# Redrawing the order of batch 0's scores, exponentials and global products in a hand-written list

## The chip, the cores and the metric

The kernel runs on one core of one Trainium2 chip. The metric is device time in microseconds; the kernel before is told by the median of five runs. A separate execution was taken with the hardware profiler, and every view of a profile below is of that one execution.

## The reference, cut to what matters

An attention of a Longformer kind is followed by an MLP of a ResMLP kind. There are 8 batches of 576 tokens, 8 heads of 64, and 8 global tokens. Every token sees the tokens within 32 of it and the global ones; a global token sees all.

```python
def _attn_ref(q, k, v, global_idx):
    scores = scale * np.matmul(q, k.transpose(0, 1, 3, 2))
    mask = np.abs(pos[:, None] - pos[None, :]) <= window      # window = 32
    mask = mask | is_global[:, None] | is_global[None, :]
    scores = np.where(mask, scores, -1000000000.0)
    ...                                                       # softmax
    return np.matmul(attn, v)

def _moe_ref(x, alpha1, beta1, w_tok, alpha2, beta2, w_ch1, w_ch2, lam):
    a1 = alpha1 * x + beta1
    tok = np.einsum('ts,bsd->btd', w_tok, a1)
    u = x + lam * tok
    a2 = alpha2 * u + beta2
    ch = np.maximum(a2 @ w_ch1, 0.0) @ w_ch2
    return u + lam * ch
```

## The kernel before, in words

The work falls into batches for the attention and into nine groups of 512 rows for the MLP. From the first MLP group on, matmuls of the MLP are the base of TensorE's program and the attention and token mixing of later batches are woven in between. Batch 0 has no MLP to be woven into. Its whole attention, its token mixing, and much of the loading and filling are drawn in one order written out by hand: the string `FIRST` (line 45), a list of words. A loop (line 1025) goes through the words and issues each word's instructions at once. Each engine runs its own instructions in the order of the list; a wait arises wherever an operand or a PSUM bank isn't ready. A word with a colon names the PSUM bank (0 to 7) that it writes.

Heads are worked in four pairs, 0 to 3; "third pair" is pair 2. The words, with the pair as a digit `h`:

- `z{h}{u}:bank` only names a bank; `s{h}{u}:bank` issues the score matmuls of half `u` (`sc0_mm`, line 353) into that bank and the one of `z`: ten matmuls for `u` 0, eight for `u` 1. The first half needs windows 0 to 4, the second 5 to 8.
- `e{h}{u}{a}`: the exponential on ScalarE (line 364) of head `a` of the pair, 344 columns for `u` 0, 272 for `u` 1.
- `gk1:bank`, `gk0:bank`: scores of the global keys against all queries of the four pairs (`gk0_mm`, line 300), four matmuls each; `eg1`, `eg0`: their exponentials (line 306); `G`: two VectorE products (line 278) that make the rows `G` from these and the mask `GM`. `GMa`, `GMb` fill that mask (line 857).
- `pg{h}`: two VectorE products (line 326) that pick the global queries' probabilities from the exponentials; `pt{h}`: two more (line 333) that mask the window's probabilities. Both need all four exponentials of the pair.
- `q{h}:bank`: the global query product, five matmuls (line 381); `ra{h}` on ScalarE (line 386) and `rd{h}` on VectorE (line 390) turn its result into `RG`.
- `pvx{h}`, `pvy{h}`: the PV matmuls of query tiles 0 to 2 and 3 to 4 (`pv_mms`, line 403). Each output starts with a matmul of `G` and `RG`. `nx{h}`, `ny{h}`: their normalisation on VectorE (lines 422 and 429) or, for some pairs, `nr` and `ny` on VectorE and ScalarE (line 459). `xl{h}`, `xm{h}`: scaling by alpha and lambda, on GpSimd but for pair 3 (lines 447, 464 and 465).
- `va1`, `vb1`, `va2`, `vb2`: VectorE copies of V to an odd offset (lines 936 to 939).
- `la` (GpSimd, line 963), `lb:bank` (two float32 matmuls), `lc` (ScalarE, line 965): the row lambda times alpha, spread over the partitions. The scaling needs `lc`.
- `ab:bank`, `abe`: a transpose of eight rows (line 907) and three small VectorE copies (lines 915 to 917).
- `wt{k}:bank`, `we{k}`: transposes of the token weight (line 869) and their copies by ScalarE (line 873). `rs:bank`, `re`: the token weight's row sums, which need all five.
- `sp:n`: n spare matmuls into bank 7, whose result nobody reads (line 821).
- `qtt` and `ktt`: copies of the last 64 tokens' queries (VectorE, line 684) and keys (ScalarE, line 674), which a pair's second half and `gk1` need. `b1t`: two loads of batch 1 issued by GpSimd; `pz0`, `v1f`, `qz0`, `qz1`: fills on GpSimd; `u0`: a load of batch 1's V issued by GpSimd; `beta`: a product of one row on GpSimd (line 863).

The word lists are turned into instructions by these lines:

```python
for w in FIRST.split():
    n, _, b = w.partition(":")
    if n == "sp":
        spare(int(b))
    elif b:
        hb[n] = banks[int(b)]
        ops[n](hb[n])
    else:
        ops[n]()
```

Of the kernel before, what the change touches and what calls it, by code (L numbers as in the profile page):

```python
# [44 lines left out]
FIRST = """  # L45
kgz vez io ktz pgz gb1 gbm:0 W0 gbc ar0 pz1 ar1 gath ck0 ar2 pgc tk0:1 sp:3 cq0 mask idn tq0:2 sp:16 V0 pz3
qv0 V1 pz2 cq1 V2 tq1:3 kt0 cq2 V3 tq2:4 sp:1 ck2 qv1 qv2 ck1 ck3 tk2:5 V4 kt2 tk1:6 wki cq3 gat1 kt1 tk3:0 wi
kt3 gx tq3:2 ct qv3 gt:1 tt:3 sp:3 ge0 ge1 gte fz ktt GMa qtt z20:4 s20:5 gk1:6 e201 e200 z21:0 z11:2 s11:1
gk0:3 b1t la eg1 va1 GMb s21:5 e111 z00:4 s00:6 eg0 z10:1 sp:2 va2 e210 s10:3 vb1 e211 z01:0 sp:2 e001 s01:5
e100 lb:6 e011 pz0 e010 pg2 G z31:1 s31:5 lc v1f qz0 qz1 u0 pt2 ab:0 abe sp:2 e310 q2:6 e000 wt1:1 ra2 wt3:4  # L50
sp:2 we1 pg0 rd2 pvx2:6 e101 vb2 pt0 e311 pvy2:1 e110 q0:3 nx2 we3 wt0:5 pg1 ra0 wt2:2 nr2 ny2 we0 wt4:6 xl2
rd0 we2 q1:4 pt1 z30:1 s30:5 pvx0:3 we4 xm2 pvy0:2 nx0 ra1 rs:6 e300 beta rd1 e301 nr0 pg3 pvy1:1 re pvx1:3
ny0 pt3 xl0 q3:4 tm2:5 ra3 nr1 ny1 kc0 kc1 rd3 xm0 u1 nx1 pvy3:6 pvx3:2 ad2 xl1 tm0:4 nx3 xm1 u2 u3 u4 nr3 ad0
ny3 qc0 qc1 tx2:3 tm1:5 xl3 xm3 tx0:4 ad1 bm0 tm3:6 ut0 ut2 tx1:5 ad3 ut1 bm1 bm2 tx3:4 gc1 ut3 kc2 kc3 b1i
qc2 qc3 bm3 W1s bme
"""
PLACE = {t: (g, j) for g, ts in enumerate(GROUPS) for j, t in enumerate(ts)}

# [1091 lines left out]
```

## Time and profile before

| what | value |
|---|---|
| median of 5 runs | 390.28 us (386.78 to 391.09) |
| profiled execution, its own time | 388.55 us |
| its span | 386.6 us |
| TensorE busy | 374.9 us, 97% of the span |
| VectorE busy | 227.8 us, 59% |
| ScalarE busy | 175.2 us, 45% |
| GpSimd busy | 206.8 us, 53% |
| first matmul of the MLP | at 38.67 us |
| mean granted TensorE clock | 0.996 |

PE is TensorE, PEld its weight loads, DVE VectorE, ACT ScalarE, POOL GpSimd and SP SyncE. In a row of a timeline the first number is the start and the second the time from the first start to the last end of the instructions merged in it; their count is behind the x. What stands in brackets at the end is the idle time of the engine before them and what ended it. Instructions of one engine overlap at their ends, so that the next can start before the row is over.

### The profile page before, as it was taken

The numbers are of one execution on the slowest core, as the hardware profiler recorded it, in microseconds if no ns is written. First come the engines' busy times: TensorE is split into PE (matmuls) and PEld (weight loads), VectorE is DVE, ScalarE is ACT, GpSimd is POOL, SyncE is SP. The second block draws the span as 40 slices with busy tenths as digits, with TensorE's granted clock in tenths as the row PEclk, the third lists the DMA queues.
The fourth block names the chain that finished last, engine by engine and source line by source line (L and its number), as shares of the span: only waits on it lengthen the run. The fifth ranks groups of instructions, "written<-read, shape, count | busy, mean of one in ns | idle before, by whom it ended". The sixth has DMA issues, their size and how long they took to land.

```text
span 386.6 us, 8189 instructions
## 1 busy us (share of the span) xinstructions
PE 374.9 (97%) x3120; PEld 209.2 (54%) x3120; DVE 227.8 (59%) x589; ACT 175.2 (45%) x350; POOL 206.8 (53%) x268
## 2 busy tenths in 40 slices
PE   6799999999999999999999999999999999999996
PEld 4469565546654665456545664466456654444443
DVE  6988567984477557945595559545864554014023
ACT  6786874008800881067305740386028700731720
POOL 7988647289458944894388647963241345000000
PEclk9899999999999999999999999999999999999999
DMA  8999999959979994999497999799240013101002
GB/s 258 179 228 265 211 182 153 195 81 172 140 144 137 142 167 98 117 158 144 110 128 130 146 145 104 128 151 146 82 110 1 3 56 81 42 20 62 29 27 81
DMA packets 160836, 47.87 MB, mean 124 GB/s; under 512 B 147537, under 2 KB 154521, under 8 KB 160798
## 3 DMA queue, kind: packets, MB, share of 16 engines
q0 software_dynamic: 98288, 17.05, 63.1%
q1 hardware_dynamic: 61518, 29.18, 35.7%
q10 hardware_dynamic: 992, 1.13, 1.0%
q8 instruction: 24, 0.39, 0.4%
q14 instruction: 14, 0.11, 0.1%
HBM read 38.90 MB, written 9.44 MB: 125 GB/s over the span
## 4 chain that ended last, share of the span: by engine, by line
PE 88%; DVE 7%; ACT 3%; issue 1%; POOL 1%; ACTq 0%; DVEq 0%
PE bank L127 86%; DVE XR L583 1%; DVE OT L582 1%; POOL UB L508 1%; DVE QP L239 1%; DVE XR L429 1%; ACT UT L621 1%; ACT KT L639 1%; DVE XR L503 1%; PE bank L635 0%; PE bank L901 0%; ACT HT L567 0%; DVE QP L645 0%; ACT L742 0%; DVE PGQ L326 0%
## 5 line engine op out<-in xcount | busy, mean ns | idle before, releaser
L127 PE MATMUL bank<-UT,W 128*128 128x512 bf16 x576 | 159.3, 379 | 0.0
L127 PE MATMUL bank<-W,HT 128*128 128x512 bf16 (+2 forms) x592 | 140.1, 373 | 0.0
L567 ACT ACTIVATE HT<-bank,bias 128x512 bf16<-128x512 f32 x128 | 87.9, 687 | 52.3 <-PE bank L127 51.5
L368 ACT ACTIVATE E<-bank 128x416 f16<-128x416 f32 (+1 forms) x84 | 41.8, 513 | 114.7 <-PE bank L127 113.9
L127 PEld LDWEIGHTS <-HT 128*128 128x128 bf16 (+1 forms) x610 | 54.4, 98 | 53.8 <-issue 1.9
L447 POOL TENSOR_TENSOR XL<-XR,LA 128x384 bf16<-128x384 f32 x29 | 29.1, 1003 | 74.1 <-DVE XR L429 52.2
L127 PEld LDWEIGHTS <-W 128*128 128x128 bf16 (+1 forms) x658 | 51.6, 97 | 25.5
L582 DVE TENSOR_TENSOR OT<-bank,LAM 128x512 f32<-128x512 f32 (+2 forms) x37 | 24.9, 673 | 53.8 <-PE bank L127 53.6
L508 POOL TENSOR_TENSOR UB<-XR,A 128x512 bf16<-128x512 f32 x28 | 35.8, 1288 | 24.9 <-DVE XR L503 14.3
L127 PE MATMUL bank<-RG,G 128*128 128x65 f16 x320 | 42.9, 193 | 1.3 <-DVE RG L390 1.3
L127 PE MATMUL bank<-XL,wtT 128*128 128x512 bf16 (+2 forms) x240 | 41.6, 326 | 0.0
L127 PE MATMUL bank<-Ve,PT 128*128 128x65 f16 x300 | 41.1, 194 | 0.0
L127 PEld LDWEIGHTS <-PT 128*128 128x128 f16 x540 | 30.8, 98 | 17.5 <-issue 1.1
L127 PEld LDWEIGHTS <-G 128*128 128x128 f16 x320 | 30.7, 97 | 15.2 <-DVE RG L390 0.9
L127 PEld LDWEIGHTS <-KT 128*128 128x128 bf16 (+1 forms) x324 | 23.4, 100 | 20.2 <-issue 3.5
L223 POOL DMA_DIRECT2D Ve<-in_v_dram x40 | 34.2, 877 | 0.2
L127 PE MATMUL bank<-Vo,PT 128*128 128x65 f16 x240 | 33.4, 192 | 0.0
L216 POOL DMA_DIRECT2D Kb<-in_k_dram x30 | 27.0, 899 | 4.0 <-DMA W<-in_moe_w_ch_dram 3.9
L127 PE MATMUL bank<-QP,KT 128*128 128x144 bf16 (+1 forms) x252 | 28.7, 223 | 0.4 <-DVE QP L251 0.3
L216 POOL DMA_DIRECT2D Qb<-in_q_dram x30 | 26.8, 895 | 4.2 <-DMA W<-in_moe_w_ch_dram 3.7
L583 DVE TENSOR_TENSOR XR<-OT,XR 128x512 f32<-128x512 f32 (+2 forms) x33 | 27.3, 827 | 1.6
L127 PEld LDWEIGHTS <-wtT 128*128 128x128 bf16 (+1 forms) x240 | 18.7, 99 | 17.6 <-issue 1.7
(160 smaller groups left out, 413.8 us busy)
## 6 DMA issues: line engine op xcount, KB each, us to landing
out_dram<-XR SPq DMA_DIRECT2D x31, 256.0 KB
W<-in_moe_w_ch_dram POOLq DMA_DIRECT2D x4, 1024.0 KB, 15.1
Vo<-Ve SPq DMA_DIRECT2D x12, 260.0 KB
Ve<-in_v_dram POOLq DMA_DIRECT2D x24, 128.0 KB, 5.2
Kb<-in_k_dram POOLq DMA_DIRECT2D x24, 128.0 KB, 6.4
Qb<-in_q_dram POOLq DMA_DIRECT2D x24, 128.0 KB, 6.4
Ve<-in_v_dram POOLq DMA_DIRECT2D x16, 96.0 KB, 5.1
XR<-in_k_dram SPq DMA_DIRECT2D x2, 512.0 KB
```

Of the source, the lines that this page charges most:

```text
L127: nc.tensor.matmul(out=o, lhsT=l, rhs=r, start=st, stop=sp, skip_group_check=True)
L216: nc.gpsimd.dma_start(out=dst[0:n, c, :].rearrange("p (h d) -> p h d", d=D), in_=src[b, :, c * P : c * P + n, :].rearrange("h p d -> p h d"))
L223: nc.gpsimd.dma_start(out=Ve[b % 2][r0 : r0 + hi - lo, c, :, 0:D], in_=v[b, :, lo:hi, :].rearrange("h p d -> p h d"))
L239: nc.vector.tensor_copy(out=QP[r, hp, a, :, 0:64], in_=QT[r, hp, 0:S].rearrange("p (t j) -> p t j", j=64))
L368: nc.scalar.activation(out=eb(b, hp)[:, UOFF[u] : UOFF[u + 1]], in_=ps[:, 0:n], func=AF.Exp, bias=0.0, scale=0.125)
L429: nc.vector.tensor_tensor(out=xo, in0=pv[:, :, :, 0:64], in1=rb, op=ALU.mult)
L447: xl_eng(b, hp).tensor_tensor(out=XL[b % 2][:, 0:3, cs], in0=XR[:, base : base + 3, cs], in1=lb, op=ALU.mult)
L503: nc.vector.tensor_tensor(out=x, in0=ps, in1=x, op=ALU.add)
L508: nc.gpsimd.tensor_tensor(out=ub, in0=x, in1=A2, op=ALU.mult)
L567: nc.scalar.activation(out=HT[:, ec, :], in_=st[ec], func=AF.Relu, bias=b_, scale=1.0)
L582: nc.vector.tensor_tensor(out=ot, in0=ps, in1=LAM[:, lo:hi], op=ALU.mult)
L583: nc.vector.tensor_tensor(out=x, in0=ot, in1=x, op=ALU.add)
```

## The change

Only the list `FIRST` is changed, between `s20` and the transposes of the token weight. The third pair's second half of scores is drawn ahead of the global keys' scores, and its exponentials, `pg2`, `q2`, `ra2` and `rd2` ahead of the other pairs' later work; its PV is drawn ahead of `lb`, `ab` and the token weight's transposes. The first half of pair 1's scores moves up behind `s20`. Several words have other banks. The spare matmuls of this part are five instead of eight. From `wt0` on, the list is the same but for `nr2` and `ny2`, which now stand earlier.

```diff
-kt3 gx tq3:2 ct qv3 gt:1 tt:3 sp:3 ge0 ge1 gte fz ktt GMa qtt z20:4 s20:5 gk1:6 e201 e200 z21:0 z11:2 s11:1
-gk0:3 b1t la eg1 va1 GMb s21:5 e111 z00:4 s00:6 eg0 z10:1 sp:2 va2 e210 s10:3 vb1 e211 z01:0 sp:2 e001 s01:5
-e100 lb:6 e011 pz0 e010 pg2 G z31:1 s31:5 lc v1f qz0 qz1 u0 pt2 ab:0 abe sp:2 e310 q2:6 e000 wt1:1 ra2 wt3:4
-sp:2 we1 pg0 rd2 pvx2:6 e101 vb2 pt0 e311 pvy2:1 e110 q0:3 nx2 we3 wt0:5 pg1 ra0 wt2:2 nr2 ny2 we0 wt4:6 xl2
-rd0 we2 q1:4 pt1 z30:1 s30:5 pvx0:3 we4 xm2 pvy0:2 nx0 ra1 rs:6 e300 beta rd1 e301 nr0 pg3 pvy1:1 re pvx1:3
+kt3 gx tq3:2 ct qv3 gt:1 tt:3 sp:3 ge0 ge1 gte fz ktt GMa qtt z20:4 s20:5 e201 e200 z10:0 s10:2 e101 e100 b1t
+la z21:6 s21:1 va1 e211 e210 GMb gk1:5 eg1 gk0:4 eg0 va2 pg2 z11:0 s11:2 e111 e110 vb1 z00:6 s00:1 q2:3 ra2 G
+e001 e000 z01:5 s01:4 pt2 rd2 pz0 sp:2 pvx2:0 vb2 pvy2:2 e011 e010 z31:6 s31:1 v1f e311 e310 nx2 nr2 ny2 lb:3
+lc ab:5 abe pg0 qz0 qz1 u0 sp:3 wt1:0 wt3:4 we1 pt0 we3 q0:3 wt0:5 pg1 ra0 wt2:2 we0 wt4:6 xl2 rd0 we2 q1:4
+pt1 z30:1 s30:5 pvx0:3 we4 xm2 pvy0:2 nx0 ra1 rs:6 e300 beta rd1 e301 nr0 pg3 pvy1:1 re pvx1:3 ny0 pt3 xl0
```

More of the change, by code (lines that the diff above doesn't have):

```diff
@@ L47 @@
 qv0 V1 pz2 cq1 V2 tq1:3 kt0 cq2 V3 tq2:4 sp:1 ck2 qv1 qv2 ck1 ck3 tk2:5 V4 kt2 tk1:6 wki cq3 gat1 kt1 tk3:0 wi
-kt3 gx tq3:2 ct qv3 gt:1 tt:3 sp:3 ge0 ge1 gte fz ktt GMa qtt z20:4 s20:5 gk1:6 e201 e200 z21:0 z11:2 s11:1
-gk0:3 b1t la eg1 va1 GMb s21:5 e111 z00:4 s00:6 eg0 z10:1 sp:2 va2 e210 s10:3 vb1 e211 z01:0 sp:2 e001 s01:5
-e100 lb:6 e011 pz0 e010 pg2 G z31:1 s31:5 lc v1f qz0 qz1 u0 pt2 ab:0 abe sp:2 e310 q2:6 e000 wt1:1 ra2 wt3:4
-sp:2 we1 pg0 rd2 pvx2:6 e101 vb2 pt0 e311 pvy2:1 e110 q0:3 nx2 we3 wt0:5 pg1 ra0 wt2:2 nr2 ny2 we0 wt4:6 xl2
-rd0 we2 q1:4 pt1 z30:1 s30:5 pvx0:3 we4 xm2 pvy0:2 nx0 ra1 rs:6 e300 beta rd1 e301 nr0 pg3 pvy1:1 re pvx1:3
-ny0 pt3 xl0 q3:4 tm2:5 ra3 nr1 ny1 kc0 kc1 rd3 xm0 u1 nx1 pvy3:6 pvx3:2 ad2 xl1 tm0:4 nx3 xm1 u2 u3 u4 nr3 ad0
-ny3 qc0 qc1 tx2:3 tm1:5 xl3 xm3 tx0:4 ad1 bm0 tm3:6 ut0 ut2 tx1:5 ad3 ut1 bm1 bm2 tx3:4 gc1 ut3 kc2 kc3 b1i
-qc2 qc3 bm3 W1s bme
+kt3 gx tq3:2 ct qv3 gt:1 tt:3 sp:3 ge0 ge1 gte fz ktt GMa qtt z20:4 s20:5 e201 e200 z10:0 s10:2 e101 e100 b1t
[3 more added lines that the diff above has]
+pt1 z30:1 s30:5 pvx0:3 we4 xm2 pvy0:2 nx0 ra1 rs:6 e300 beta rd1 e301 nr0 pg3 pvy1:1 re pvx1:3 ny0 pt3 xl0
+q3:4 tm2:5 ra3 nr1 ny1 kc0 kc1 rd3 xm0 u1 nx1 pvy3:6 pvx3:2 ad2 xl1 tm0:4 nx3 xm1 u2 u3 u4 nr3 ad0 ny3 qc0 qc1
+tx2:3 tm1:5 xl3 xm3 tx0:4 ad1 bm0 tm3:6 ut0 ut2 tx1:5 ad3 ut1 bm1 bm2 tx3:4 gc1 ut3 kc2 kc3 b1i qc2 qc3 bm3
+W1s bme
 """
```

## The prediction

> **What bounds the kernel now.** I read the page first, then the chain that ended last, then a table of windows cut at the edges of the slow stretch of the clock, then the timelines of TensorE, VectorE and GpSimd from 13 to 30 us, where the change lies. The page and the chain say that TensorE is the end-setter nearly everywhere:
>
> ```profile
> span 386.6 us, 8189 instructions
> PE 374.9 (97%) x3120; PEld 209.2 (54%) x3120; DVE 227.8 (59%) x589; ACT 175.2 (45%) x350; POOL 206.8 (53%) x268
> ...
> PE 88%; DVE 7%; ACT 3%; issue 1%; POOL 1%; ACTq 0%; DVEq 0%
> ```
>
> So only TensorE's idle or half-clock time can be won, and a delay on another engine counts only where TensorE runs dry. From 100 us on, TensorE is busy 283.2 of 286 us, and nothing there is edited; a shift made before 30 us should travel to the end roughly one for one. What the edited stretch looks like is in the windows (first column start:end, then its length, then busy time of PE, PEld, DVE, ACT, POOL with instruction counts, then granted clock):
>
> ```profile
> 11.52:14.93 3.41, 1.91 (x25) 1.26 (x23) 3.09 (x9) 2.26 (x7) 3.30 (x11) 0.99 2.91 148
> 14.93:18.35 3.42, 3.42 (x44) 1.65 (x44) 3.19 (x5) 1.96 (x6) 3.40 (x5) 0.51 1.21 213
> 18.35:21.76 3.41, 3.41 (x51) 2.06 (x48) 2.30 (x11) 2.88 (x9) 3.19 (x8) 1.00 1.06 219
> 21.76:25.17 3.41, 2.99 (x65) 2.61 (x63) 3.19 (x13) 3.41 (x9) 2.17 (x3) 1.00 1.06 229
> ```
>
> A slice in which TensorE is busy 1.91 of 3.41 us (56%) is followed by one at half clock; slices at 2.9 of 3.41 (86%) are not. The reader should also see that VectorE has 2.3 to 3.2 of 3.4 us of work: it is the second bound. TensorE's gaps are few:
>
> ```profile
> 14.70 1.10 PE L127 MATMUL bank<-W,KGP 128*128 128x320 bf16 x4 [1.12 <-DVE W L684]
> ...
> 24.31 0.41 PE L869 MATMUL bank<-C,HT 96*64 96x96 bf16 x6 [0.36 <-DVE XR L429]
> ...
> 27.99 0.20 PE L127 MATMUL bank<-RG,G 128*128 128x65 f16 x1 [0.44 <-DVE RG L390]
> ```
>
> VectorE decides each of them:
>
> ```profile
> 14.68 0.71 DVE L936 COPY Vo<-Ve 64x1560 f16<-64x1560 f16 x1
> ...
> 16.50 1.59 DVE L937 COPY Vo<-Ve 64x1560 f16<-64x1560 f16 x1
> 18.26 0.31 DVE L326 TENSOR_TENSOR PGQ<-W,gqm 128x80 f16<-128x80 f16 x2 [0.17 <-ACT W L364]
> 18.49 0.82 DVE L278 TENSOR_TENSOR G<-EG,GM 128x1024 f16<-128x1024 f16 x2
> 19.23 0.82 DVE L333 TENSOR_TENSOR HT<-W,mask 128x640 f16<-128x640 f16 x2
> ...
> 28.18 1.27 DVE L326 TENSOR_TENSOR PGQ<-W,gqm 128x80 f16<-128x80 f16 x2
> ```
>
> The copy vb1 (L937) takes 1.59 us where its twin va1 (L936) takes 0.71, and the same pair of L326 products takes 0.31 or 1.27. The long ones lie under tensor products on GpSimd (`la`, 16.41 to 17.67 us; L447, 27.98 to 28.98 us).
>
> **The change, part by part.** No instruction is new; three of the eight spare matmuls of this stretch go. GpSimd's own order (b1t, la, pz0, v1f, qz0, qz1, u0, xl2) is the same before and after, and so is SP's: b1t's two DMAs and u0's are moved in the list, but past nothing on their queue. What is reordered is TensorE, ScalarE and VectorE.
>
> (1) s10 into the gap. Pair 1's first ten score matmuls (18.20 to about 18.48) go right behind s20, whose matmuls start at 13.07 and take 0.51. They need only what s20 needed, so they run at 13.4 to 13.9, inside the 1.12 us gap. s21 then takes the place of gk1 at 14.70, behind the same copy (qtt, L684). Gain on TensorE 0.3.
>
> (2) Scores of pair 2 ahead of the global keys. s21's eight matmuls at full clock are done by 15.05; the exponentials go at the steps seen on ScalarE (0.35 for 344 columns, 0.28 for 272): e201 at 13.88, e200, e101, e100, then e211 at 15.28, e210 done at 15.95 instead of about 18.2. gk1 and gk0 follow at 14.92 to 16.9 (their own 1.07 and 0.9 at half clock), so eg0 ends at 17.4 instead of 17.5.
>
> (3) VectorE. va1, GMb, va2 stay and end at 16.48. pg2 now comes before vb1, and starts at 16.50 under `la`. Its cost is 0.31 to 1.27 by the two rows; vb1 then has 0.71 of work, of which the row of 1.59 shows that about 0.3 gets done in 1.17 us under `la`. Either way vb1 ends at 18.1 to 18.4, which is where it ended before (18.09). So G starts at 18.2 to 18.45 (18.49 before) and pt2 ends at 19.8 to 20.05 (20.05 before). **This is the step at which the gain goes**: e210 is over 2 us earlier, yet G and pt2 are not, for VectorE's queue was the later one.
>
> (4) TensorE to the PV. s11 and s00 take 16.85 to 17.9, q2 0.5 at half clock to 18.4, s01 and sp:2 to 18.95. ra2 (0.37) is done at 18.9, rd2 follows pt2 and ends at 20.1 to 20.4. pvx2's first matmul waits for rd2, and all of TensorE behind it: s31, lb, ab, wt1. New idle time 1.15 to 1.45 us, where there was none. The PV starts at 20.1 to 20.4 instead of 22.15.
>
> (5) From the PV to pair 0's PV. Start-to-start steps of the rows of before: pvx2 and pvy2 0.85, s31 0.23, lb 1.05, ab 0.16, sp:3 0.48, wt1 and wt3 0.61, q0 0.27, wt0 and wt2 0.61, wt4 0.35, q1 0.47, s30 0.33: 5.41 in all. So pvx0 comes at 25.5 to 25.8, against 25.46. The 0.36 gap before wt4 is gone, since pvx2 no longer shares bank 6 with it. ScalarE adds a little: its five wide weight copies (0.53 each) now start at about 23.6 behind wt1, not at 21.58, so we4 ends at 26.35 to 26.8, and rs, which needs it, starts at 26.5 to 26.85 instead of 26.31. That is 0.2 to 0.55 late. Behind rs, TensorE before waited 0.44 us for rd1, which hides most of this; ScalarE's `re` and ny0 end up to 0.5 later.
>
> (6) VectorE behind it. nx2 and ny2 (about 1.45 together) now run at 20.9 to 22.6, but pg0 waits for abe, abe for ab, ab for lb: pg0 at 22.8 to 23.1, pt0 to 24.7 at worst, rd0 (behind ra0 and the late we1, we3) at 24.85 to 25.2, against 25.11. xl2 on GpSimd starts at about 23.2 instead of 24.43, so it lies under pt0, and `beta` lies under pt1 as xm2 did. pt1, nx0, rd1 and pg3 come out where they were, within 0.25 us.
>
> **Sum.** TensorE: 1.12 gap mostly filled, 0.36 gap removed and 0.4 of spares gone, but idle 1.3 new, and pair 0's chain 0 to 0.55 later: I take +0.3, the middle. Against the profiled execution's own 388.55 us (span 386.6 and 1.95 around it) that is 388.85. The median of the five runs is 1.73 above that execution, so on the scale of the runs 390.28 + 0.3 = 390.6. The runs spread by 4.3 us, or 1.1%; so about 1% (3.9 us) is what such a measurement can tell from no change.
>
> **The clock.** The unknown is whether the new 1.3 us stall makes a second half-clock slice. In 18.35 to 21.76 TensorE would be busy about 2.0 of 3.41 us (58%), next to the 56% that was punished and far from 86% that was not. The price is bounded by 0.17, the wait that the present half-clock slice shows on VectorE, and 1.71, half of 3.41, if TensorE sets the end throughout; lb, ab and the transposes are a chain through TensorE, so I take 1.4. On the other side s10 raises the first slice from 1.91 to about 2.3 busy; if it then stays at full clock, little is won, since vb1 on VectorE ends at 18.1 anyway.
>
> The Trainium skill ("TensorE: Matmul & The Clock Gate", section on HAM oscillation) speaks of TensorE gaps over about 3.4 us as what sends the clock down. This trace disagrees: its longest gap is 1.12 us and the clock still halved. By the page the new stall would be free of it, and the sum would stay at 390.6; by the row it may be 392.0.
>
> **Rivals.**
> A, forecast, chance 0.50: the stall moves and nothing is won: 390.6, own range 389.4 to 391.9 (0 to 0.55, with nearly 1 us for the median of five).
> B, slower, 0.27: the stall at 18.95 to 20.3 sends the clock to half from 21.8 to 25.2. For it: 58% against 56%. Against: the threshold may be just between, and the slices start at a different place in each run. It decides once rd2 comes later than about 20 us. 390.6 + 1.4 = 392.0, at most 392.4.
> C, faster, 0.16: vb1 and pg2 are not stretched by `la`, so vb1 ends at 17.55, G and pt2 come 0.6 to 0.9 earlier, and rs comes at 25.9. For it: va1's 0.71. Against: `la` starts behind b1t at 16.41 in both. The weight copies then also come early: 390.6 - 1.1 = 389.5.
> D, it doesn't do what it says, 0.07: rd2 is held until 22.1, so the PV isn't earlier, and the lb, s31 and transposes behind it are later: 22.15 + 5.41 = 27.56 for pvx0, 2.1 late: 392.4.
>
> The range takes in B's upper end and C with the spread of a median: 388.3 to 393.4. Over 1% needs a second cause on top (two extra slow slices, or a disturbed stretch after 40 us): 0.13 slower, from B and D; 0.06 faster, from C; 0.81 within.
>
> **What would show it.** A TensorE gap of over 1 us ahead of the first RG,G matmul, released by RG L390, with that matmul at 20.1 to 20.4; G at 18.2 to 18.5; the L873 copies starting at about 23.6; rs (wtT,ones) at 26.5 to 26.9; q3 within 0.5 of 29.50. Half clock at 21.8 to 25.2 is B. G before 17.9 is C. I am wrong if W1's first MLP matmul (38.67) moves by over 2 us, or if it doesn't and the time does.

## The result, and the profile after

The changed kernel takes 391.21 us (median of 38 runs, 389.68 to 393.49), the kernel before 388.89 us (median of 75 runs beside these). The ratio is 1.0054, 95% interval 1.0041 to 1.0067: slower by some 2.1 us, clear of noise and within 1%. (The difference of the medians is 2.3; the ratio is not the quotient of the medians.) The forecast of 390.6 stood on the five runs known then, whose median of 390.28 was 1.4 above that of the 75; as a difference it was +0.3, and +2.1 came.

The head of the page of the changed kernel, profiled execution 391.94 us:

```profile
span 390.0 us, 8182 instructions
PE 375.9 (96%) x3117; PEld 210.6 (54%) x3117; DVE 228.8 (59%) x589; ACT 175.4 (45%) x350; POOL 207.3 (53%) x268
```

The span is 3.4 us longer, and TensorE's busy time only 1.0, with three matmuls fewer. TensorE's timeline shows where it stood still:

```profile
15.88 0.61 PE L127 MATMUL bank<-W,KT 64*128 64x64 bf16 x18
18.47 0.44 PE L127 MATMUL bank<-Ve,PGQ 128*128 128x130 f16 x5 [1.98 <-DVE PGQ L326]
18.85 0.30 PE L127 MATMUL bank<-W,KT 64*128 64x64 bf16 x8
19.08 0.39 PE L127 MATMUL bank<-C 128*128 128x256 bf16 x2
20.97 0.21 PE L127 MATMUL bank<-RG,G 128*128 128x65 f16 x1 [1.50 <-DVE RG L390]
...
30.98 1.24 PE L127 MATMUL bank<-wtT,ones 128*128 128x512 bf16 x5
...
42.19 1.02 PE L127 MATMUL bank<-UT,W 128*128 128x512 bf16 x4
```

In the kernel before, the PV and rs stood here:

```profile
22.15 0.19 PE L127 MATMUL bank<-RG,G 128*128 128x65 f16 x1
...
26.31 1.24 PE L127 MATMUL bank<-wtT,ones 128*128 128x512 bf16 x5
```

The PV (RG,G) starts at 20.97 instead of 22.15, earlier as it should. But ahead of it stand two gaps, 1.98 us in front of q2 and 1.50 us in front of the PV, where the kernel before had none. Then rs starts at 30.98 instead of 26.31 and the MLP at 42.19 instead of 38.67. So 1.2 us were won at the PV and 5.9 lost between the PV and rs, in these two executions. The windows, cut at the edges of the slow stretch, say how (columns as before):

```profile
16.82:20.24 3.42, 1.00 (x15) 0.68 (x16) 3.28 (x8) 1.77 (x7) 3.31 (x7) 1.00 1.17 216
20.24:23.65 3.41, 2.68 (x37) 2.27 (x37) 2.70 (x9) 0.95 (x4) 3.21 (x4) 0.50 1.07 224
23.65:27.07 3.42, 3.42 (x24) 2.16 (x22) 1.99 (x8) 1.46 (x4) 1.31 (x2) 0.50 1.04 225
27.07:30.48 3.41, 3.41 (x47) 2.85 (x46) 2.74 (x6) 3.32 (x8) 2.05 (x3) 0.50 1.14 240
30.48:33.89 3.41, 3.41 (x69) 2.66 (x67) 2.80 (x9) 1.87 (x7) 1.43 (x2) 1.00 1.33 272
```

TensorE is busy 1.00 of 3.42 us in the slice with the gaps, and the next three slices, 10.2 us, run at half clock. The kernel before had one such slice. Below, a slice of 3.4 us at half clock is called a slow slice. In the profiled executions a mean clock of 0.995 or 0.996 goes with one slow slice, 0.991 with two, 0.985 with three and 0.982 with four. VectorE's timeline, last, shows what TensorE waited for:

```profile
15.65 0.64 DVE L936 COPY Vo<-Ve 64x1560 f16<-64x1560 f16 x1 [1.04 <-DMA Ve<-in_v_dram]
...
16.89 1.11 DVE L938 COPY Vo<-Ve 64x520 f16<-64x520 f16 x1 [0.16 <-DMA Ve<-in_v_dram]
18.01 0.31 DVE L326 TENSOR_TENSOR PGQ<-W,gqm 128x80 f16<-128x80 f16 x2
...
19.02 0.83 DVE L278 TENSOR_TENSOR G<-EG,GM 128x1024 f16<-128x1024 f16 x2
...
20.62 0.30 DVE L390 SCALAR_TENSOR_TENSOR RG<-bank,RG 32x130 f16<-32x130 f32 x1
```

The exponentials of pair 2 were over at 16.1. pg2 stood behind va1, GMb and va2 on VectorE until 18.01, and G came at 19.02, later than before (18.49).

### The profile page after: what moved, and what is told of

It is laid out like the page before. It is cut to its first block, busy times and chain, and to the rows that moved or that the text cites. A ratio compares the mean times of both kernels' runs of the same rounds, so it can differ in the third digit from the quotient of the medians.

```text
span 390.0 us, 8182 instructions
## 1 busy us (share of the span) xinstructions
PE 375.9 (96%) x3117; PEld 210.6 (54%) x3117; DVE 228.8 (59%) x589; ACT 175.4 (45%) x350; POOL 207.3 (53%) x268
## 4 chain that ended last, share of the span: by engine, by line
PE 91%; DVE 3%; DMA 2%; POOL 1%; ACT 1%; issue 1%; DVEq 0%
PE bank L127 90%; DMA Ve<-in_v_dram 2%; POOL Ve L223 1%; PE bank L869 1%; POOL KQG L255 1%; PE bank L901 0%; ACT HT L567 0%; DVE QP L645 0%; ACT E L364 0%; DVE XL L465 0%; DVE XR L429 0%; DVE XR L583 0%; PE bank L635 0%; DVE OT L582 0%; PE bank L270 0%
## 5 line engine op out<-in xcount | busy, mean ns | idle before, releaser
L127 PE MATMUL bank<-RG,G 128*128 128x65 f16 x320 | 43.9, 195 | 2.6 <-DVE RG L390 2.6
```

The source lines that it names most:

```text
L127: nc.tensor.matmul(out=o, lhsT=l, rhs=r, start=st, stop=sp, skip_group_check=True)
```

## The experiments

Theory 1: the gaps send the granted clock to half, and that is the loss. Theory 2: the order itself costs, with lb, ab and the weight copies behind the PV. Theory 3, formed after the first four runs: VectorE's products, moved next to GpSimd's, stretch. Each run's mean granted clock is known, so times can be sorted by it. "Before" in the table is all 105 runs of it beside the experiments, in three sets of 35.

| kernel | median us | ratio to before (95%) | runs at clock 0.994 and more | median of the runs at 0.998 and more |
|---|---|---|---|---|
| before | 388.6 to 388.9 | 1 | 78 of 105 | 388.28 (34 runs) |
| after | 391.21 | 1.0054 (1.0041 to 1.0067) | 0 of 40 | none |
| spares in the gaps | 389.28 | 0.9993 (0.9961 to 1.0024) | 11 of 12 | 389.17 (9) |
| lb ahead of q2 | 390.67 | 1.0040 (1.0012 to 1.0067) | 1 of 12 | none |
| both | 391.70 | 1.0060 (1.0030 to 1.0089) | 4 of 12 | 390.00 (2) |
| s10 alone, in before | 388.68 | 0.9983 (0.9955 to 1.0011) | 11 of 12 | 387.81 (4) |
| lb in the second gap | 391.42 | 1.0062 (1.0034 to 1.0090) | 3 of 12 | none |
| spares, xl2 late | 390.32 | 1.0023 (0.9994 to 1.0052) | 12 of 12 | 390.04 (10) |
| lb in gap, xl2 late | 389.92 | 1.0018 (0.9987 to 1.0050) | 12 of 13 | 389.90 (7) |
| before, no spares | 388.91 | 0.9997 (0.9969 to 1.0025) | 1 of 12 | none |
| spares, products out | 388.27 | 0.9996 (0.9971 to 1.0020) | 12 of 12 | 388.07 (11) |
| before, products out | 387.76 | 1.0003 (0.9964 to 1.0042) | 7 of 12 | 387.26 (3) |
| spares, products and la out | 388.00 | 0.9975 (0.9947 to 1.0003) | 12 of 12 | 387.34 (10) |
| products first | 388.50 | 0.9992 (0.9967 to 1.0016) | 12 of 12 | 388.61 (7) |

The last column is coarse. For the kernel before it is 388.30, 387.33 and 388.29 in the three sets, so a difference of less than 1 us in it is a hint and no more.

**Spares in the gaps.** Only matmuls that nobody reads are added to the changed list:

```diff
-... vb1 z00:6 s00:1 q2:3 ra2 G
+... vb1 z00:6 s00:1 sp:14 q2:3 ra2 G
-e001 e000 z01:5 s01:4 pt2 rd2 pz0 sp:2 pvx2:0 ...
+e001 e000 z01:5 s01:4 pt2 rd2 pz0 sp:14 pvx2:0 ...
```

> The changed kernel with 14 more spare matmuls ahead of q2 and 12 more ahead of pvx2, where TensorE stood idle for 2.0 and 1.5 us. Nothing else moves. Theory 1 (the loss is the half clock that follows these gaps): three slow slices become one or none, the mean granted clock goes from 0.982-0.991 to 0.994 or more, and the time falls from 391.2 to about 389.4, a ratio to the kernel before of 1.001. Theory 2 (the loss is the order itself: lb, ab and the weight copies stand behind the PV, whatever the clock): the clock may rise, but the time stays within 0.4 us of the changed kernel, ratio 1.004 to 1.006.

391.21 became 389.28, as theory 1 had it, and 11 of 12 runs kept a clock of 0.994 or more, where none of the changed kernel's 40 did. No real work was moved or removed, so the 1.9 us are the clock's; the intervals of the two ratios don't overlap. The changed kernel's own 40 runs point the same way: their median is 390.33 at a clock of 0.989 to 0.991 (9 runs), 391.35 at 0.985 to 0.987 (19) and 391.78 below (12). That settles theory 1 as the larger part. But at full clock the run with spares is still 0.9 slower than the kernel before at full clock. (The kernel before has slow slices in many runs too, so 1.9 and 0.9 don't add up to the loss.) Its profiled execution, one of the three of 12 below 0.998, shows a new gap later. First TensorE, then VectorE, then GpSimd, from their timelines:

```profile
27.21 0.72 PE L127 MATMUL bank<-Ve,PGQ 128*128 128x130 f16 x5 [2.45 <-DVE PGQ L326]
```

```profile
23.14 2.73 DVE L333 TENSOR_TENSOR PT<-E,mask 128x640 f16<-128x640 f16 x2
25.79 1.36 DVE L326 TENSOR_TENSOR PGQ<-E,gqm 128x80 f16<-128x80 f16 x2
```

```profile
23.74 1.02 POOL L447 TENSOR_TENSOR XL<-XR,LA 128x384 bf16<-128x384 f32 x1
```

pt0 takes 2.73 us (0.83 before, the row below) and pg1 1.36 (0.30): they now lie under xl2, xm2 and beta.

```profile
22.61 0.83 DVE L333 TENSOR_TENSOR PT<-E,mask 128x640 f16<-128x640 f16 x2
```

The slow slice starts at 27.14, behind this gap; whether the nine runs at full clock have the gap too, no trace shows.

**lb ahead of q2, alone and with spares.**

```diff
-... z00:6 s00:1 q2:3 ra2 G
+... z00:6 s00:1 lb:2 q2:3 ra2 lc G          (with spares: sp:8 lb:2 ..., and sp:10 ahead of pvx2)
-... nx2 nr2 ny2 lb:3 lc ab:5 abe ...
+... nx2 nr2 ny2 ab:5 abe ...
```

> The changed kernel with lb and lc drawn ahead of q2 again, in bank 2, so that 1.05 us of real work fills a part of the first gap and leaves the chain behind the PV. Theory 1 (half clock): at most one slow slice fewer, so the mean clock stays under 0.993, and about 0.7 us comes back from the clock beside up to 1 us from the shorter chain; ratio to before 1.001 to 1.003. Theory 2 (order): the chain from pvx2 to wt1 is 1.05 us shorter (2.07 at half clock) whatever the clock does; ratio 1.000 to 1.003. The clock tells them apart, and e1 beside it.

> lb and lc ahead of q2 as in e2, with eight spare matmuls ahead of lb and eight more ahead of pvx2: both gaps filled and the chain short. Theory 1: clock 0.994 or more, time 388.4 to 388.9, ratio 0.998 to 1.000. Theory 2: as e2, within 0.3 us of it. If the two causes add, this is the only one of the three that reaches the kernel before.

Both missed, the second in full: 391.70. The waits of TensorE in the first of the two say why (its profiled execution is the one run of 12 at a clock of 0.996):

```profile
PE bank L127 <- POOL LA L963: 3.0, 1, 3.0
```

lb waited for GpSimd's row `la`, and q2 with all that follows stood behind lb. A gap was filled with an instruction that has a wait of its own. With the spares, that wait was 0.4 us in the profiled execution, but TensorE waited 2.7 for pg0 and pg1; most runs there have a slow slice.

**s10 alone.** In the list of before, `z10:0 s10:2 e101 e100` goes behind `e201 e200`, and these words' old places go.

> The kernel before with one part of the change alone: the first half of pair 1's scores and its two exponentials drawn right behind s20 and e200 (banks 0 and 2). The prediction gave this part 0.3 us on TensorE, and it fills 0.3 of the 1.12 us gap that precedes the one slow slice of the kernel before. Theory 1: clock 0.996 or a little over, 0 to 0.7 us faster, ratio 0.998 to 1.000. Theory 2, by which order alone counts: VectorE sets G and pt2, so nothing is won, ratio 1.000 within 0.001.

388.68, ratio 0.9983 with 1 inside the interval: theory 1's 0 to 0.7 us and theory 2's none can't be told apart here.

**lb in the second gap; xl2 late; both.**

```diff
 # lb in the second gap, with sp:14 ahead of q2
-e001 e000 z01:5 s01:4 pt2 rd2 pz0 sp:2 pvx2:0 ...      lb:3 lc ab:5
+e001 e000 z01:5 s01:4 lb:2 pt2 rd2 pz0 lc sp:6 pvx2:0 ...   ab:5
 # xl2 late, with sp:14 ahead of q2 and of pvx2
-... qz0 qz1 u0 sp:3 ...
+... qz0 qz1 u0 u1 u2 sp:3 ...
```

> The changed kernel with 14 spare matmuls ahead of q2 (as in the run with spares) and lb in bank 2 behind s01, lc ahead of pvy2, six spares ahead of pvx2 instead of two: the second gap is filled with 1.05 us of real work, and unlike the run with lb ahead of q2 nothing stands behind the wait for la. Theory 1 (the clock alone is the loss): the time is that of the run with spares, 389.3, as the clock is full in both. Theory 3 (beside the clock, lb and ab behind the PV push pg0 and pt0 on VectorE under the GpSimd products of xl2): ab and pg0 come 1 us earlier, pt0 is over before xl2 starts on GpSimd at about 23.7 and takes 0.8 us instead of 2.7, and the time is 387.6 to 388.4, ratio to before 0.996 to 0.999.

> The run with spares (14 ahead of q2, 12 more ahead of pvx2) with the GpSimd loads u1 and u2 of batch 1 drawn ahead of xl2, so that xl2, xm2 and beta start some 1.7 us later on GpSimd, at about 25.4. Nothing moves on the other engines. Theory 3 (VectorE's products stretch under GpSimd's): pt0 takes 0.8 to 1.0 us instead of 2.7 and pg1 0.3 instead of 1.4, but pt1 falls under xl2 and xm2 as in the kernel before; the gap of 2.5 us ahead of q1 goes; time 388.2 to 388.8 against 389.3 with spares alone. Theory 1 (clock alone): 389.3, unchanged.

> lb in the second gap as in e5, and u1 and u2 ahead of xl2 as in e6. Theory 3: the two remove the same stretch of pt0 and pg1, so little beyond the better of them, 387.4 to 388.3; if pt1 is moved clear of xm2 too, up to 0.8 more. Theory 1: 389.3.

All three missed. With lb in the gap, lc is early, and xl2 starts on GpSimd as soon as it is free; VectorE's pg0 falls under it. VectorE, then GpSimd:

```profile
22.90 1.86 DVE L326 TENSOR_TENSOR PGQ<-E,gqm 128x80 f16<-128x80 f16 x2
24.68 2.19 DVE L333 TENSOR_TENSOR PT<-E,mask 128x640 f16<-128x640 f16 x2
```

```profile
23.24 1.01 POOL L447 TENSOR_TENSOR XL<-XR,LA 128x384 bf16<-128x384 f32 x1
```

q0 then waits 1.69 us, and 9 of 12 runs are at a clock of 0.991. With xl2 late the clock is full (12 of 12), and yet the time is 1.0 above spares alone: pt0 takes 1.62 us at 23.75 to 25.37 while u0 to u2 are issued (22.58 to 25.17), and pt1 2.12 under xm2 and beta. The collision had only moved. These runs don't contradict theory 3, but don't prove it: the times that it gave for them did not come.

**Before without its spares.** The eight `sp:2` matmuls of the stretch are dropped from the kernel before.

> The kernel before without the eight spare matmuls of the edited stretch; the change took three of them away and opened gaps. Theory 1: TensorE's slices get emptier by up to 0.9 us in all, more runs show three or four slow slices (mean clock 0.982 to 0.991) and the median rises to 389.5 to 391, ratio 1.002 to 1.005. Theory 2 (order alone): the spares are idle work, and without them the time is the same or 0.2 us less, ratio 0.999 to 1.000.

The clock fell as theory 1 expected (1 of 12 runs at 0.994 and more), and the time did not move: 388.91, not the 389.5 to 391 of theory 1. The spares cost about what they save there. So a lower clock is not always a net loss. That it costs only where TensorE's work ends last is an argument; this run doesn't show it, since dropping the spares also freed TensorE.

**The products out, as a test of theory 3.** xl2, xm2 and beta are replaced by fills of the same tiles, which leaves pair 2's scaled rows and a row of beta out of the token mixing; in the third kernel la too.

```diff
 def scale_x(b, hp):
     ...
+    if (b, hp) == (0, 2):
+        return fill(XL[0][:, 0:3, cs], 0.0, nc.gpsimd)
 ...                                   # scale_y likewise
-"beta": lambda: b0_beta(0, g_),
+"beta": lambda: fill(XL4[0][64:65, :], 0.0, g_),
```

> The run with spares (14 ahead of q2, 12 more ahead of pvx2), and GpSimd's products xl2, xm2 and beta replaced by fills of the same tiles with zeros, so that pair 2's scaled rows and one row of beta are left out of the token mixing. Theory 3 (VectorE's products stretch under GpSimd's work): pt0, pg1 and pt1 fall to 0.8, 0.3 and 0.8 us, the gap ahead of q1 goes, and the time is 387.4 to 388.2 against 389.3 with spares alone. Theory 1 (the clock is the whole loss): 389.3, unchanged. That the fills stretch VectorE as the products do would show in pt0, and leave the time at 389.3 too.

> The control: the kernel before with the same three products replaced by fills, the same parts left out. There only pt1 (1.34 us) lay under them. Theory 3: 0.2 to 0.6 us faster, 388.2 to 388.7; the distance to the run with spares and fills is then 0.7 us or less in its favour or none. Theory 1: unchanged, 388.9.

> As the run with spares and fills, and la replaced by a fill too, so that the row lambda times alpha is left out as well. This is the step on which the prediction let the gain go: pg2, va2 and vb1 lie under la. If that is right, pg2 takes 0.3 us, va2 0.33 and vb1 0.7, rd2 and the PV come 0.6 to 0.9 earlier (19.5 to 19.9), and the time falls by 0.3 to 0.9 against that run. If va1, va2 wait for the loads of V instead, the PV stays at 20.3 to 20.8 and the time where it was.

VectorE with spares and fills, then GpSimd's fills, which start as pt0 ends:

```profile
22.84 0.82 DVE L333 TENSOR_TENSOR PT<-E,mask 128x640 f16<-128x640 f16 x2
23.58 0.31 DVE L326 TENSOR_TENSOR PGQ<-E,gqm 128x80 f16<-128x80 f16 x2
```

```profile
23.71 1.30 POOL L615 MEMSET XL<- 128x384 bf16 x4
```

pt0 is back at 0.82 us and pg1 at 0.31, and TensorE's gap ahead of q1 is gone. No fill lies beside pt0 here. The same execution has both cases a little earlier: G under the product `la`, and pt2 under the fills behind it. VectorE, then GpSimd:

```profile
16.77 1.90 DVE L278 TENSOR_TENSOR G<-EG,GM 128x1024 f16<-128x1024 f16 x2
18.59 0.81 DVE L333 TENSOR_TENSOR HT<-W,mask 128x640 f16<-128x640 f16 x2
```

```profile
17.02 1.55 POOL L968 TENSOR_TENSOR LA<-LA,UB 1x512 f32<-1x512 f32 x1
18.53 0.62 POOL L615 MEMSET PT<- 128x640 f32 x1
19.10 1.01 POOL L615 MEMSET Ve<- 32x260 f32 x3
```

G takes 1.90 us where it took 0.83 in the changed kernel, behind `la`; pt2 takes 0.81 under fills. So the stretch is real and comes from the products and not from fills.

What it costs is less sure. The median fell from 389.28 to 388.27, and at full clock from 389.17 to 388.07, but the ratios to the kernel before beside each, 0.9993 and 0.9996, don't show it. The fills also keep GpSimd busy for 1.3 us where the products took 3.3, and they need neither nx2 nor lc, which is not separated from the stretch. About 1 us is thus a reading of the runs at full clock. The control forbids more: the kernel before, with the same products out, also loses about 1 us at full clock (388.28 to 387.26, three runs only; its ratio is 1.0003, since five of its 12 runs have the lowest clock). Both pay for this collision, so it doesn't explain the 0.9 us by which the changed order stays behind at full clock. What these consist of is open.

With la out as well, the median of the runs at full clock is 0.7 us lower (387.34 against 388.07), inside the expected 0.3 to 0.9. But these runs fall into two groups, six at 387.0 to 387.4 and four at 388.6 to 389.6, and the means differ by 0.3 only, so the gain is not clear. And in the profiled execution va2 still took 1.08 us and pg2 came at 17.82, so that a gain runs over those instructions is not shown either.

**Products first**, the version meant to beat both: lb and lc in the second gap, sp:14 ahead of q2, pg0, pt0, pg1, pt1 and rd0 ahead of nx2, u0 behind beta, ab in bank 7.

```diff
+e001 e000 z01:5 s01:4 lb:2 pt2 rd2 pz0 lc sp:4 pvx2:0 vb2 e011 e010 pvy2:2 pg0 pt0 z31:6 s31:1 v1f e311 e310 ab:7
+q0:3 pg1 ra0 pt1 wt1:4 wt3:5 we1 wt0:6 we3 wt2:1 we0 q1:4 rd0 nx2 we2 nr2 ny2 qz0 qz1 pvx0:3 wt4:0 xl2 abe ra1 xm2
+pvy0:2 we4 nx0 z30:1 s30:5 rs:6 e300 beta u0 rd1 e301 nr0 pg3 pvy1:1 re pvx1:3 ...
```

> A version meant to beat both: the changed list with 14 spares ahead of q2, lb and lc in the second gap, and pg0, pt0, pg1, pt1 and rd0 drawn ahead of nx2 on VectorE, so that they are over before xl2, which waits for nx2, starts on GpSimd; u0 goes behind beta; ab in bank 7; the banks of the weight transposes are dealt out anew. Theory 3: pg0 to pt1 at 21.4 to 23.5 in 2.1 us, pvx0 at about 24 instead of 25.5 to 27, rs at about 25.9 (ScalarE's wide copies set it), full clock: 387.2 to 388.4, ratio 0.995 to 0.999. Theory 1: as the run with spares, 389.3.

```profile
21.78 0.31 DVE L326 TENSOR_TENSOR PGQ<-E,gqm 128x80 f16<-128x80 f16 x2
22.01 0.82 DVE L333 TENSOR_TENSOR PT<-E,mask 128x640 f16<-128x640 f16 x2
22.74 0.30 DVE L326 TENSOR_TENSOR PGQ<-E,gqm 128x80 f16<-128x80 f16 x2
22.96 0.82 DVE L333 TENSOR_TENSOR PT<-E,mask 128x640 f16<-128x640 f16 x2
```

pg0 to pt1 run in 2.0 us, unstretched, within 0.4 us of the place foreseen, and pvx0 comes at 24.28. 388.50, ratio 0.9992 (0.9967 to 1.0016), just above the range given: it undoes the loss of the change and does not beat the kernel before, nor the spares alone (0.9993). Its spread is small (387.57 to 389.03). TensorE now waits 1.1 us in sum, later, for GpSimd's scaled rows (lines 447, 464 and 465) ahead of the token mixing, since u0 and later xl2 have pushed GpSimd's queue back.

## Why the prediction was right and wrong

**Right on the range, lucky in the number.** Within 1%, a little slower, and inside the range. But +0.3 was forecast and +2.1 came; that 390.6 lies only 0.6 from 391.21 is luck, since the five runs under it were 1.4 too high. The reason given for the range's upper end, rival B, is what happened; the forecast itself, A, is not. The prediction's own signs say so: in the profile the first MLP matmul moved by 3.5 us, from 38.67 to 42.19, where over 2 was to mean that it is wrong, q3 came at 33.03, not within 0.5 of 29.50, rs at 30.98, not 26.5 to 26.9, and the half clock lay at 20.25 to 30.48. Only the gap ahead of the PV came about as said (1.50 us, released by rd2), with the PV at 20.97, not 20.1 to 20.4.

**Step 1** held: in the profile s10 runs behind s20, and the gap ahead of s21 is 0.42 us instead of 1.12. What it is worth alone wasn't resolved.

**Steps 2 and 3** held in their mechanism: e210 was done at 16.1 (15.95 foreseen), 2 us earlier, and G came no earlier, because VectorE's queue was the later one. The size was off by 0.6 us: G at 19.02, not 18.2 to 18.45. In this execution va1 waited 1.04 us for a load of V, which the working had left out, and va2 took 1.11 instead of 0.33. Nor does `la` alone explain the 1.59 us of vb1 in the kernel before, as the working read it: with spares vb1 took 0.56 beside `la`, which had started 0.05 us behind it. What stretches the copies is open.

**Step 4 is the term that was mis-sized.** One gap of 1.15 to 1.45 us was foreseen and 1.98 + 1.50 = 3.5 us came. The working ran gk1 to s00 at the half clock of the profiled execution of before, so that TensorE would reach q2 at 17.9, just as pg2 was ready. In the changed kernel that stretch ran at full clock: s00 was over at 16.5 and TensorE stood until 18.47. Some 1.4 us of the first gap are this; the other 0.6 is pg2, late as step 3 says. The prediction did ask what comes if the clock stays full there and answered that little is won; it didn't ask where TensorE would then stand idle. The place of a slow slice in one execution had been taken as fixed.

**Step 5 and B's price.** At full clock the walk was nearly right: from pvx2 to rs 6.4 us were foreseen (20.4 to 26.85); with spares and the products out, at full clock, they took 26.22 - 19.79 = 6.43, and with the products in but late, at full clock too, 27.95 - 20.78 = 7.17. In the changed kernel, at half clock, they took 30.98 - 20.97 = 10.0. The price of B was put at 1.4 and at most 1.71 for one slice; three came in the profiled execution (the mean clocks of the 40 runs, 0.977 to 0.991, speak for two or more in each), and the spares brought 1.9 us back. The chances (0.50 for A, 0.27 for B) rested on 58% busy in the slice with the stall; it was 29%.

**Step 6** failed in the part that didn't decide. pt0 was allowed 1.34 us, the longest row of before; in the profiled execution with spares it was 2.73, in the changed kernel 1.62. Since the kernel before pays for the same products about as much, this is not what keeps the run with spares at 389.2.

Rival C's condition came true and its gain did not: pg2 took 0.31 us and vb1 0.63, both behind `la`, but vb1 ended at 18.99, not 17.55, because of the load of V and of va2's 1.11 us. Whether `la` stretched va2 is open, since it took 1.08 with `la` out. Rival D was wrong: the PV did come earlier.

**The clock rule.** In the changed kernel the clock halved behind gaps of 2.0 and 1.5 us. In the kernel before, the gap ahead of the slow slice was 1.12 us. (It is the longest there, not of the whole trace, as the prediction has it: TensorE's first matmul came after 2.75 us.) The Trainium skill ("TensorE: Matmul & The Clock Gate", section on why this matters for your kernels) tells to avoid gaps of more than about 3 us; these traces disagree: shorter gaps were enough. By that rule B would have been left out.

## What to carry to other kernels

Where a matmul is moved ahead, look first at which queue releases it: here the exponentials came 2 us earlier and VectorE's queue, not they, set the product. Never price a step by a clock that one execution happened to have; price the same stretch at full and at half clock, and ask where TensorE then stands idle. A gap is best filled with work that has no wait of its own: spare matmuls brought back 1.9 us, and real work that waited for GpSimd brought back 0.5 at most.

## What the runs showed of the hardware

- The clock fell to half after slices of 3.4 us in which TensorE was busy 29% (after), 30% (spares, 23.72 to 27.13), 56% (before), 59% (lb in the second gap, 21.11 to 24.52) and 62% (s10 alone, 2.13 of 3.41 us from 16.54), and not after one of 2.08 in 3.42 us, 61% (after, 10.01 to 13.43). So the border is near 60%, and this share alone doesn't settle it. The clock came back after one slice in the kernel before, two with lb in the second gap, three in the changed kernel and four in the kernel before with the products out, though TensorE was busy throughout the later ones; why is open.
- Two products of VectorE on float16 tiles stretched from 0.82 to 2.73 us under GpSimd's tensor products (pt0 with spares) and stayed at 0.81 under GpSimd's fills (pt2 with spares and products out). The normalisations, which read PSUM, kept their 0.56 and 0.29 us under such products (before, at 27.04 under beta and at 24.60 under xl2). The Trainium skill ("GPSIMD Engine Reference", section Specifications) says that GpSimd's SBUF interfaces are shared with VectorE and collide with its instructions that have two SBUF inputs; the runs agree, with a factor of up to 3.3.
- A kernel's median hides the clock: 21 of 105 runs of the kernel before had a mean clock under 0.988 and a median of 392.2 us, against 388.3 at full clock.
